# Decayed keys in a buffer of their own, made one chunk ahead of the scores

## The chip, the core and the metric

The kernel runs on one core of one Trainium2 chip. The metric is device time in microseconds (us). A kernel is timed in several runs, and the median counts. One more run is profiled; its rows are quoted below. Engines are named as the profile names them: PE (TensorE, matmuls) with PEld (its weight loads), DVE (VectorE), ACT (ScalarE), POOL (GpSimd) and SP (SyncE, which issues most of the DMAs).

## What is computed

Three stages follow one another: a linear attention with a decaying state, a dense feed-forward layer with SiLU, and a mixture of 8 experts of which each token takes one.

```python
def _attn_ref(q, k, v, alpha):            # batch 4, heads 8, seq 768, head_dim 48
    for t in range(S):
        state = alpha[:, :, t, :, None] * state + np.einsum('bhd,bhe->bhde', k[:, :, t], v[:, :, t])
        y[:, :, t] = np.einsum('bhd,bhde->bhe', q[:, :, t], state)

def _moe_ref(x, w_in, w_out):             # 3072 tokens, 384 -> 2048 -> 384
    h = x @ w_in
    return (h * (1.0 / (1.0 + np.exp(-h)))) @ w_out

def _moe2_ref(...):                       # token -> one of 8 experts, relu(x @ w1[e]) @ w2[e], times its gate
```

## The kernel before

The attention is cut into 24 chunks. Chunk n holds 128 positions of one of the 4 batches, for all 8 heads; n // 4 is the place in the sequence and n % 4 the batch. The feed-forward layer is cut into 8 blocks of 384 tokens, so a block uses the output of 3 chunks. Block 0 can start when its chunks are there, and from then on the attention of later chunks is mixed into the feed-forward work: `block` calls `pump_j` twice for each of the 16 pieces of a block, and each call takes one step of the generator `att_steps`. After the last block come the experts.

Matrix products of this kernel are made from two fp16 halves of each operand (a high part and a rest), three products for each pair; `qs`, `ss`, `vs`, `st` and `kd` are such pairs. The high part is a copy on ACT, the rest a subtraction on DVE or POOL.

A chunk n goes through these steps. `att_A` makes the running product P of the decays and its reciprocal R on DVE, and the end decay `pe` on POOL. `att_Bk` transposes k on PE into the PSUM tile `ptr` and multiplies it by R into `K` (L673, DVE). `att_Bq` does the like for `Q`, and splits it into `qs`. `att_C` makes the scores: 16 small matmuls `sc<-Q,K` (L717), copied to `S` by ACT (L727) and masked by POOL (L728). `att_S` splits the masked scores into `ss` (L740 on ACT, L741 on DVE). `att_KT` prepares the keys for the state: for chunks from `NF` = 6 on it multiplies `K` in place by the end decay (L754, POOL), splits the product into `kd` (L756 on ACT, L757 on POOL) and lets a DMA transpose it into `KT` (L759, queue of SP). `att_D` makes the output `yp` from `ss` and `vs` (L795) and from `qs` and the old state (L788). `att_U` makes `up<-vs,KT` (L829) and adds it to the state (L843, DVE). The last 4 chunks (20 to 23) need no new state, so `att_KT` and `att_U` return at once there.

Steps of two chunks are interleaved: after `att_C(n)` follow `att_A(n+1)`, `att_S(n)` with `att_KT(n)`, `att_Bk(n+1)`, `att_D(n)`, `att_Bq(n+1)` and `att_U(n)`.

The PSUM tiles of attention (`sc` twice, `ptr` three times, `yp`, `up`, so 7 for a chunk) take turns in 3 banks of the pool `ps_a`. The bank of `up` is that of the transposed k, so `up` of chunk n waits until `K` of chunk n+1 has been multiplied; the bank of the transposed q is that of the transposed decays, which R reads.

The order on each engine isn't the order of the code: a list scheduler places the instructions of all engines by its own estimate of when each could run. Each engine then works through its list in that order. The feed-forward matmuls are L900 (`mm1`) and L923 (`mm2`). `lead["a"]` is the latest ACT instruction that made the fp16 copy of a feed-forward piece; `behind(x, y)` holds x after y on the same engine.

At the end of a block `route` finds the expert of each token (many small DVE operations, a few on POOL, and a scatter by POOL, L990).

Of the kernel before, what the change touches and what calls it, by code (L numbers as in the profile page):

```python
# [8 lines left out]
FP32 = mybir.dt.float32  # L9
FP16 = mybir.dt.float16  # L10
I32 = mybir.dt.int32
ACTF = mybir.ActivationFunctionType
ALU = mybir.AluOpType
# [259 lines left out]
def attention_silu_moe_kernel(  # L273
# [14 lines left out]
    nc = tc.nc  # L288
    B, H, S, D = q.shape
# [4 lines left out]
    NPAIR = H // 2  # L294
    NCH = NT // 128
# [27 lines left out]
    def guard(kind, thr=0.0, op=ALU.is_lt):  # L323
# [16 lines left out]
        out=tri, in_=tri, pattern=[[1, 128]], compare_op=ALU.is_gt, fill=0.0, base=0, channel_multiplier=-1  # L340
# [32 lines left out]
    if True:  # L373
# [54 lines left out]
        NBUF, NF = 2, 6  # L428
# [52 lines left out]
        def behind(ins, before):  # L481
            tc.add_manual_dep(
                ins.ins, before.ins.name, mybir.DependencyInfo(mybir.DependencyClass.NoSync, mybir.DependencyReason.DATA),
                reason="an order within one engine",
            )
# [45 lines left out]
        gates, lead = {}, {}  # L531
# [94 lines left out]
        def att_load(n, names):  # L626
            if n >= NCH:
                return
            c, b = divmod(n, B)
            for nm in names:  # L630
                t = third[nm] if n == 2 else nat[nm][n % NBUF]
                nc.sync.dma_start(
                    out=t[:, :, 0:D], in_=att_src[nm][b, :, c * 128:(c + 1) * 128, :].rearrange("h p d -> p h d")
                )
                ch.setdefault(n, {})[nm] = t
# [4 lines left out]
        def transpose4(src):  # L640
            pt = bank([128, NPAIR, 128], FP32, "ptr")
            for p in range(NPAIR):
                nc.tensor.transpose(pt[:, p, :], src[:, p * 128:(p + 1) * 128], ident)
            return pt
# [24 lines left out]
        def att_Bk(n):  # L669
            d = ch[n]  # L670
            pk = transpose4(flat(d["k"]))
            K = a2.tile([128, NPAIR, 128], FP32, tag="K", name="K")
            ins = nc.vector.tensor_mul(out=K, in0=pk, in1=d["R"])  # L673
            if n == 2:
                lead[0] = ins
            d["K"] = K

# [65 lines left out]
        def att_KT(n):  # L743
            d = ch[n]
            if n // B == CPB - 1:
                return
            K = d["K"]
            if n < NF:
                pk = transpose4(K.rearrange("p a t -> p (a t)"))
                KT = d["KT"] = a2.tile([128, NPAIR, 128], FP32, tag="KT", name="KT32")  # L750
                nc.scalar.activation(out=KT, in_=pk, func=ACTF.Copy)
                return
            wide = d["pe"][:, 0].rearrange("r (p o) -> r p o", o=1).to_broadcast([128, NPAIR, 128])
            nc.gpsimd.tensor_tensor(out=K, in0=K, in1=wide, op=ALU.mult)  # L754
            kd = a2.tile([128, 2, NPAIR, 128], FP16, tag="kd", name="kd", bufs=1)
            nc.scalar.activation(out=kd[:, 0], in_=K, func=ACTF.Copy)  # L756
            nc.gpsimd.tensor_sub(out=kd[:, 1], in0=K, in1=kd[:, 0])  # L757
            KT = a2.tile([128, 2 * NPAIR, 128], FP16, tag="KT", name="KT")
            nc.sync.dma_start_transpose(out=KT, in_=kd.rearrange("p s a t -> p (s a t)"))  # L759
            d["KT"] = KT  # L760

        THREE = ((0, 0), (0, 1), (1, 0))

        def att_D(n, g):
            d = ch[n]
            c, b = divmod(n, B)
            if g == 0:
                d["y"] = bank([128, 512], FP32, "yp")[:, 0:H * D]
            yp = d["y"]
            if n >= NF:  # L770
                vs, ss = d["vs"], d["ss"]
            for p in (2 * g, 2 * g + 1):
                w = 2 * D * p
                if n < NF:
                    if c:
                        nc.tensor.matmul(
                            out=yp[:, w:w + 2 * D], lhsT=d["Q"][:, p, :], rhs=state[b][:, p, :], start=True, stop=False
                        )
                    for i in range(2):
                        cs = slice(w + i * D, w + (i + 1) * D)  # L780
                        nc.tensor.matmul(
                            out=yp[:, cs], lhsT=d["S"][i][:, p, :], rhs=flat(d["v"])[:, cs], start=(c == 0),
                            stop=(c == 0 or i == 1),
                        )
                    continue
                if c:
                    for m, (x, y) in enumerate(THREE):
                        nc.tensor.matmul(  # L788
                            out=yp[:, w:w + 2 * D], lhsT=d["qs"][:, x, p, :], rhs=d["st"][:, y, p, :],
                            start=(m == 0), stop=False,  # L790
                        )
                for i in range(2):
                    cs = slice(w + i * D, w + (i + 1) * D)
                    for m, (x, y) in enumerate(THREE):
                        nc.tensor.matmul(  # L795
                            out=yp[:, cs], lhsT=ss[:, i, x, p, :], rhs=vs[:, y, cs], start=(c == 0 and m == 0),
                            stop=(m == 2 and (c == 0 or i == 1)),
                        )
            if g == 1:
                ys = d["ys"] = a2.tile([128, 2, H * D], FP16, tag="ys", name="ys")  # L800
                lead[n - 1] = split(yp, SX / (SQ * SST), ys[:, 0], ys[:, 1])
# [49 lines left out]
        def att_steps():  # L851
            for n in range(3):
                att_load(n, "akqv")
            yield
            att_A(0)
            yield
            att_Bk(0)
            yield
            att_V(0)
            att_Bq(0)  # L860
            yield
            for n in range(NCH):
                more = n + 1 < NCH
                att_C(n)
                yield
                if more:
                    att_A(n + 1)
                    att_load(n + 3, "a")
                yield
                att_S(n)  # L870
                att_KT(n)
                yield
                if more:
                    att_Bk(n + 1)
                    att_load(n + 3, "k")
                    yield
                att_D(n, 0)
                yield
                att_D(n, 1)
                yield  # L880
                att_move(n)
                if more:
                    att_V(n + 1)
                    att_Bq(n + 1)
                    att_load(n + 3, "q")
                    yield
                att_U(n)
                if 0 < n < NF:
                    att_load(n + 2, "v")
                if n + 1 >= NF:  # L890
                    att_load(n + 3, "v")
                yield n
# [584 lines left out]
```

## Time and profile before

| what | us |
|---|---|
| median of 3 runs | 813.39 |
| lowest and highest run | 812.8, 814.5 |
| the profiled execution's own time | 813.08 |
| its span, first to last instruction | 811.4 |
| PE busy in the span | 753.4 |

The profiled execution took 1.7 us more than its span, which is start and end outside the instructions. In the rows below, "x16" counts instructions that a view has merged, a duration is that of the merged piece, and a bracket at the end of a row says how long the engine had stood idle before it and whose end released it. A matmul's end is modelled, and matmuls overlap: one starts while the one before it is still shown as busy.

### The profile page before, as it was taken

The numbers are of one execution on the slowest core, as the hardware profiler recorded it, in microseconds if no ns is written. First come the engines' busy times: TensorE is split into PE (matmuls) and PEld (weight loads), VectorE is DVE, ScalarE is ACT, GpSimd is POOL, SyncE is SP. The second block draws the span as 40 slices with busy tenths as digits, with TensorE's granted clock in tenths as the row PEclk, the third lists the DMA queues.
The fourth block names the chain that finished last, engine by engine and source line by source line (L and its number), as shares of the span: only waits on it lengthen the run. The fifth ranks groups of instructions, "written<-read, shape, count | busy, mean of one in ns | idle before, by whom it ended". The sixth has DMA issues, their size and how long they took to land. (4 is left out here: it accounts for less than half of the span.)

```text
span 811.4 us, 16634 instructions
## 1 busy us (share of the span) xinstructions
PE 753.4 (93%) x5614; PEld 472.3 (58%) x5614; DVE 504.3 (62%) x1452; ACT 423.9 (52%) x921; POOL 238.1 (29%) x330
## 2 busy tenths in 40 slices
PE   6788789999999899999999999989798999999996
PEld 5665467667666556665756655545354555555553
DVE  7699955587877888787887586576743222222221
ACT  2365635566766767676766675567623232222221
POOL 3351412263454554445233120030223011110101
PEclk9769979999999999999999999999899999999999
DMA  9997213044445535544431345246686666566662
GB/s 189 251 284 221 64 30 60 21 92 95 82 110 107 121 88 120 134 99 116 101 91 48 98 151 170 62 152 181 182 167 163 124 122 114 118 120 114 121 109 37
DMA packets 241100, 97.94 MB, mean 121 GB/s; under 512 B 222041, under 2 KB 230398, under 8 KB 240880
## 3 DMA queue, kind: packets, MB, share of 16 engines
q1 hardware_dynamic: 237424, 85.58, 48.6%
q0 software_dynamic: 3584, 11.18, 4.0%
q8 instruction: 51, 0.84, 0.4%
q14 instruction: 41, 0.34, 0.1%
HBM read 58.39 MB, written 12.16 MB: 87 GB/s over the span
## 5 line engine op out<-in xcount | busy, mean ns | idle before, releaser
L923 PE MATMUL o<-wo_h,w2l 128*128 128x392 f16 x528 | 147.2, 331 | 5.3 <-DVE wo_h L572 3.3
L900 PE MATMUL hp<-w2h,wi_h 128*128 128x384 f16 x576 | 145.4, 331 | 6.8 <-ACT w2l L907 3.0
L923 PEld LDWEIGHTS <-w2l 128*128 128x128 f16 x792 | 75.4, 99 | 54.7 <-issue 4.8
L1235 PE MATMUL hp<-w1h,xT 128*128 (+1 forms) x384 | 101.4, 383 | 5.5 <-DVE work L1242 5.5
L900 PEld LDWEIGHTS <-wi_h 128*128 128x128 f16 x768 | 73.8, 99 | 54.1 <-issue 9.6
L1242 DVE SCALAR_TENSOR_TENSOR work<-hp,work 128x512 f16<-128x512 f32 x56 | 38.6, 691 | 95.8 <-ACT work L1241 95.8
L900 PE MATMUL hp<-w2h,wi_l 128*128 128x384 f16 x288 | 94.2, 330 | 1.0 <-DVE wi_l L507 1.0
L923 PE MATMUL o<-wo_l,w2l 128*128 128x392 f16 x264 | 87.7, 332 | 0.0
L1235 PEld LDWEIGHTS <-xT 128*128 128x128 f16 (+1 forms) x576 | 50.4, 101 | 62.5 <-issue 8.6
L1274 POOL DMA_INDIRECT out_dram<-ob,mt x28 | 27.5, 981 | 169.6 <-ACT ob L1271 166.9
L923 PE MATMUL o<-wo_h,g 128*128 128x392 f16 x240 | 66.7, 331 | 1.7 <-ACT g L908 1.7
L1241 ACT ACTIVATE work<-hp 128x512 f16<-128x512 f32 x56 | 33.3, 596 | 61.7 <-PE hp L1235 59.9
L909 DVE SCALAR_TENSOR_TENSOR w2l<-w2l 128x384 f16<-128x384 f32 x88 | 50.7, 580 | 23.2 <-ACT w2l L908 21.9
L1235 PE MATMUL hp<-w1l,xT 128*128 (+1 forms) x192 | 64.5, 383 | 0.0
L907 ACT ACTIVATE w2l<-hp 128x384 f32<-128x384 f32 x88 | 42.2, 483 | 25.3 <-PE hp L900 21.9
L900 PEld LDWEIGHTS <-wi_l 128*128 128x128 f16 x384 | 37.8, 98 | 25.4 <-DVE wi_l L507 1.8
L923 PEld LDWEIGHTS <-g 128*128 128x128 f16 x360 | 34.5, 98 | 26.6 <-ACT g L908 2.6
L900 PE MATMUL hp<-w2l,wi_h 128*128 128x384 f16 x192 | 48.6, 326 | 0.0
L908 ACT ACTIVATE w2l<-w2l 128x384 f16<-128x384 f32 x88 | 45.3, 522 | 5.6 <-PE o L923 4.2
L1263 PEld LDWEIGHTS <-work 128*128 128x128 f16 (+1 forms) x384 | 33.3, 101 | 23.0 <-DMA work<-work 0.8
L703 POOL TENSOR_TENSOR qs<-Q,qs 128x512 f16<-128x512 f32 x18 | 21.5, 1195 | 85.0 <-ACT qs L702 85.0
L727 ACT ACTIVATE S<-sc 128x512 f32<-128x512 f32 x48 | 26.0, 593 | 35.8 <-PE sc L717 35.6
(281 smaller groups left out, 1603.1 us busy)
## 6 DMA issues: line engine op xcount, KB each, us to landing
work<-in_moe_w_dram SPq DMA_DIRECT2D x24, 512.0 KB, 3.7
work<-in_moe_w_dram SPq DMA_DIRECT2D x30, 384.0 KB, 3.3
w1h<-in_moe_w_in_dram SPq DMA_DIRECT2D x6, 768.0 KB, 5.3
nat_a<-in_alpha_dram SPq DMA_DIRECT2D x23, 192.0 KB, 3.0
nat_k<-in_k_dram SPq DMA_DIRECT2D x23, 192.0 KB, 3.7
nat_q<-in_q_dram SPq DMA_DIRECT2D x23, 192.0 KB, 3.4
nat_v<-in_v_dram SPq DMA_DIRECT2D x23, 192.0 KB, 3.0
w1h<-in_moe_w_out_dram SPq DMA_DIRECT2D x5, 768.0 KB, 8.0
```

The lines of the kernel that those rows point to most:

```text
L703: nc.gpsimd.tensor_sub(out=qs[:, 1], in0=Q, in1=qs[:, 0])
L727: nc.scalar.activation(out=s, in_=sc[i], func=ACTF.Copy, scale=SST if n >= NF else SST * SV)
L900: ins = nc.tensor.matmul(out=hp, lhsT=wi[a][f // 2][:, c, (f % 2) * 128:(f % 2 + 1) * 128], rhs=x[:, c, :], start=(n == 0), stop=(n == 3 * ...
L907: nc.scalar.activation(out=g, in_=hp, func=ACTF.Silu, scale=1.0 / (SX * SWI))
L908: lead["a"] = nc.scalar.activation(out=gh, in_=g, func=ACTF.Copy, scale=SG)
L909: lead["g"] = nc.vector.scalar_tensor_tensor(out=gl, in0=g, scalar=SG, in1=gh, op0=ALU.mult, op1=ALU.subtract)
L923: nc.tensor.matmul(out=acc[t], lhsT=a[:, ts], rhs=wo[w][f // 2][:, f % 2, :], start=(f == 0 and n == 0), stop=(f == KF - 1 and n == 2),)
L1235: nc.tensor.matmul(out=hp[ts], lhsT=xT[:, a, ts], rhs=w1s[w][c][:, e if isinstance(e, int) else bass.ds(e, 1), fs], start=(n == 0), stop=( ...
L1241: lead["a"] = nc.scalar.activation(out=hs[:, 0], in_=hp, func=ACTF.Relu)
L1242: lead["g"] = nc.vector.scalar_tensor_tensor(out=hs[:, 1], in0=hp, scalar=0.0, in1=hs[:, 0], op0=ALU.max, op1=ALU.subtract)
L1263: nc.tensor.matmul(out=po[ts], lhsT=hT[c // 4][:, at + ts.start:at + ts.stop], rhs=w2s[w][c][:, e if isinstance(e, int) else bass.ds(e, 1) ...
L1274: nc.gpsimd.indirect_dma_start(out=out[:, :], out_offset=bass.IndirectOffsetOnAxis(ap=d["row"], axis=0), in_=ob, in_offset=None, bounds_ch ...
```

## The change

`K` gets one buffer (it had two). The decayed keys get a tile `Kd` of their own instead of overwriting `K`. `att_Kd(n+1)` makes it on POOL right behind `att_Bk(n+1)`, so a chunk earlier than before. The split into `kd` and the DMA transpose (`att_kd(n+1)`) come behind the first half of `att_D(n)`, and the ACT copy in it is held behind `lead["a"]`. `att_KT` is left for the chunks below 6 alone.

```diff
--- before.py
+++ after.py
@@ -669,7 +669,7 @@
         def att_Bk(n):
             d = ch[n]
             pk = transpose4(flat(d["k"]))
-            K = a2.tile([128, NPAIR, 128], FP32, tag="K", name="K")
+            K = a2.tile([128, NPAIR, 128], FP32, tag="K", name="K", bufs=1)
             ins = nc.vector.tensor_mul(out=K, in0=pk, in1=d["R"])
             if n == 2:
                 lead[0] = ins
@@ -744,20 +744,24 @@
             d = ch[n]
             if n // B == CPB - 1:
                 return
-            K = d["K"]
-            if n < NF:
-                pk = transpose4(K.rearrange("p a t -> p (a t)"))
-                KT = d["KT"] = a2.tile([128, NPAIR, 128], FP32, tag="KT", name="KT32")
-                nc.scalar.activation(out=KT, in_=pk, func=ACTF.Copy)
-                return
+            pk = transpose4(d["K"].rearrange("p a t -> p (a t)"))
+            KT = d["KT"] = a2.tile([128, NPAIR, 128], FP32, tag="KT", name="KT32")
+            nc.scalar.activation(out=KT, in_=pk, func=ACTF.Copy)
+
+        def att_Kd(n):
+            d = ch[n]
+            Kd = d["Kd"] = a2.tile([128, NPAIR, 128], FP32, tag="Kd", name="Kd", bufs=1)
             wide = d["pe"][:, 0].rearrange("r (p o) -> r p o", o=1).to_broadcast([128, NPAIR, 128])
-            nc.gpsimd.tensor_tensor(out=K, in0=K, in1=wide, op=ALU.mult)
+            nc.gpsimd.tensor_tensor(out=Kd, in0=d["K"], in1=wide, op=ALU.mult)
+
+        def att_kd(n):
+            d = ch[n]
+            Kd = d.pop("Kd")
             kd = a2.tile([128, 2, NPAIR, 128], FP16, tag="kd", name="kd", bufs=1)
-            nc.scalar.activation(out=kd[:, 0], in_=K, func=ACTF.Copy)
-            nc.gpsimd.tensor_sub(out=kd[:, 1], in0=K, in1=kd[:, 0])
-            KT = a2.tile([128, 2 * NPAIR, 128], FP16, tag="KT", name="KT")
+            behind(nc.scalar.activation(out=kd[:, 0], in_=Kd, func=ACTF.Copy), lead["a"])
+            nc.gpsimd.tensor_sub(out=kd[:, 1], in0=Kd, in1=kd[:, 0])
+            KT = d["KT"] = a2.tile([128, 2 * NPAIR, 128], FP16, tag="KT", name="KT")
             nc.sync.dma_start_transpose(out=KT, in_=kd.rearrange("p s a t -> p (s a t)"))
-            d["KT"] = KT
 
         THREE = ((0, 0), (0, 1), (1, 0))
 
@@ -868,13 +872,19 @@
                     att_load(n + 3, "a")
                 yield
                 att_S(n)
-                att_KT(n)
+                if n < NF:
+                    att_KT(n)
                 yield
+                decayed = NF <= n + 1 < NCH - B
                 if more:
                     att_Bk(n + 1)
                     att_load(n + 3, "k")
+                    if decayed:
+                        att_Kd(n + 1)
                     yield
                 att_D(n, 0)
+                if decayed:
+                    att_kd(n + 1)
                 yield
                 att_D(n, 1)
                 yield
```

The scheduler then places the instructions anew. Line numbers behind the edit are up to 10 higher in the changed kernel.

On POOL, this is one chunk in the middle of a block (chunk 12), first before. `K<-K,pend` is the decay, `S<-S` are the two masks, `kd<-K,kd` is the rest of the split; `pend`, the state times its decay and `qs` belong to the next chunk already.

```order
L754 TENSOR_TENSOR K<-K,pend 128x512
L728 AFFINE_SELECT S<-S 128x512 x2
L664 TENSOR_SCALAR pend<-P 128x4 x2
L757 TENSOR_TENSOR kd<-K,kd 128x512
L838 TENSOR_TENSOR state_200<-state_200,pend 128x384
L703 TENSOR_TENSOR qs<-Q,qs 128x512
```

The same place in the changed kernel:

```order
L728 AFFINE_SELECT S<-S 128x512 x2
L664 TENSOR_SCALAR pend<-P 128x4 x2
L842 TENSOR_TENSOR state_200<-state_200,pend 128x384
L755 TENSOR_TENSOR Kd<-K,pend 128x512
L762 TENSOR_TENSOR kd<-Kd,kd 128x512
L703 TENSOR_TENSOR qs<-Q,qs 128x512
```

The masks now come first, and the decay and the split of the next chunk stand behind the state, ahead of `qs`.

On ACT, this is chunk 7 before; `S<-sc` are the scores, `junk` a check of P and of R, `w2l` the feed-forward pieces:

```order
L727 ACTIVATE S<-sc_1943 128x512
L727 ACTIVATE S<-sc_1944 128x512
L756 ACTIVATE kd<-K 128x512
L661 ACTIVATE junk,guard_decay<-P 128x512
L740 ACTIVATE ss<-S 128x512 x2
L661 ACTIVATE junk,guard_decay<-R 128x512
L907 ACTIVATE w2l_180<-hp 128x384
L908 ACTIVATE w2l_180<-w2l_180 128x384
L705 ACTIVATE st<-state_200 128x384
L506 ACTIVATE ys<-yp 128x384
L702 ACTIVATE qs<-Q 128x512
```

and in the changed kernel:

```order
L727 ACTIVATE S<-sc_1951 128x512
L727 ACTIVATE S<-sc_1952 128x512
L740 ACTIVATE ss<-S 128x512
L661 ACTIVATE junk,guard_decay<-P 128x512
L740 ACTIVATE ss<-S 128x512
L917 ACTIVATE w2l_180<-hp 128x384
L918 ACTIVATE w2l_180<-w2l_180 128x384
L661 ACTIVATE junk,guard_decay<-R 128x512
L761 ACTIVATE kd<-Kd 128x512
L705 ACTIVATE st<-state_200 128x384
L506 ACTIVATE ys<-yp 128x384
L683 ACTIVATE vs<-nat_v_198 128x384
```

The copy into `kd` has gone from its place ahead of both `ss` copies to one behind them, ahead of `st`, `ys`, `vs` and `qs`.

On POOL at the end of a block (behind the masks of chunk 13), where `route` (L951 to L990) is mixed in, before:

```order
L838 TENSOR_TENSOR state_201<-state_201,pend 128x384
L951 COPY row<-tok 128x1 x2
L980 TENSOR_TENSOR nx<-nx,half 128x1 x2
L974 TENSOR_SCALAR row<-nx 128x1 x2
L703 TENSOR_TENSOR qs<-Q,qs 128x512
L980 TENSOR_TENSOR nx<-nx,half 128x1
L990 DMA xs_d<-row,pos 25728x394 x2
L974 TENSOR_SCALAR row<-nx 128x1
L951 COPY row<-tok 128x1
L990 DMA xs_d<-row,pos 25728x394
```

and in the changed kernel:

```order
L842 TENSOR_TENSOR state_201<-state_201,pend 128x384
L961 COPY row<-tok 128x1 x2
L990 TENSOR_TENSOR nx<-nx,half 128x1 x2
L755 TENSOR_TENSOR Kd<-K,pend 128x512
L984 TENSOR_SCALAR row<-nx 128x1 x2
L762 TENSOR_TENSOR kd<-Kd,kd 128x512
L703 TENSOR_TENSOR qs<-Q,qs 128x512
L990 TENSOR_TENSOR nx<-nx,half 128x1
L1000 DMA xs_d<-row,pos 25728x394 x2
L984 TENSOR_SCALAR row<-nx 128x1
L961 COPY row<-tok 128x1
L1000 DMA xs_d<-row,pos 25728x394
```

Here `Kd` and the subtraction into `kd` come between the operations of `route`; the decay that stood behind the last scatter, ahead of the next masks, is gone.

On SP the transpose into `KT` stood between the loads of the decays and of k; now it stands behind the load of q. On PE no instruction is added or removed. Counted in the two orders, the feed-forward matmuls between the transposes of k and `up` are 8 or 9 in most chunks of the changed kernel and 11 in most chunks before; in chunks 9, 13, 17 and 18 they go from 11, 11, 7 and 18 to 12, 9, 14 and 23. PE's order differs from about the end of chunk 5 to the scores of chunk 20; behind these it is the same to the end of the program.

## Rows read from the trace of the kernel before

**Rows 1.** The page: PE's busy time, and its granted clock in 40 slices (tenths).

```profile
PE 753.4 (93%) x5614; PEld 472.3 (58%) x5614; DVE 504.3 (62%) x1452; ACT 423.9 (52%) x921; POOL 238.1 (29%) x330
...
PEclk9769979999999999999999999999899999999999
```

**Rows 2.** Stretches: PE, PEld, DVE, ACT, POOL busy us (instructions); clock, DMA, GB/s.

```profile
160.00:400.00 240.00, 232.27 (x2122) 156.69 (x2121) 195.77 (x529) 159.54 (x354) 114.20 (x153) 1.00 0.48 106
400.00:470.00 70.00, 70.00 (x587) 45.67 (x585) 50.38 (x146) 45.97 (x99) 16.28 (x28) 1.00 0.26 73
```

**Rows 3.** PE's waits, 160 to 400 us: us in total, times, longest.

```profile
PE up L829 <- DVE K L673: 3.1, 4, 1.1
PE pr L961 <- DVE state L843: 1.9, 2, 0.9
PE ptr L643 <- DVE R L658: 1.0, 2, 0.6
PE yp L795 <- DVE ss L741: 0.8, 1, 0.8
```

**Rows 4.** Instructions on the tile K: ns least/median/most, first and last start.

```profile
L754 POOL TENSOR_TENSOR K<-K,pend x14: 1041/1048/1751, 163.9 to 383.1; 128x512 f32<-128x512 f32 x14
...
L757 POOL TENSOR_TENSOR kd<-K,kd x14: 1149/1161/1169, 166.1 to 386.0; 128x512 f16<-128x512 f32 x14
```

**Rows 5.** Timeline of chunk 11: start us, us, instruction.

```profile
242.34 1.16 PE L717 MATMUL sc<-Q,K 64*128 64x128 f32 x16
...
243.59 1.04 POOL L754 TENSOR_TENSOR K<-K,pend 128x512 f32<-128x512 f32 x1 [2.17 <-PE sc L717]
...
243.93 0.33 PE L923 MATMUL o<-wo_h,w2l 128*128 128x392 f16 x1
...
244.26 0.49 PE L923 MATMUL o<-wo_h,w2l 128*128 128x392 f16 x2
244.59 1.23 POOL L728 TENSOR_SCALAR_AFFINE_SELECT S<-S 128x512 f32<-128x512 f32 x2
...
244.67 0.63 ACT L756 ACTIVATE kd<-K 128x512 f16<-128x512 f32 x1
...
247.10 0.62 ACT L740 ACTIVATE ss<-S 128x512 f16<-128x512 f32 x1
...
247.31 0.91 DVE L741 TENSOR_TENSOR ss<-S,ss 128x512 f16<-128x512 f32 x1
...
248.43 1.02 DVE L741 TENSOR_TENSOR ss<-S,ss 128x512 f16<-128x512 f32 x1
...
249.84 0.68 DVE L673 TENSOR_TENSOR K<-ptr,R 128x512 f32<-128x512 f32 x1
...
251.22 0.67 PE L829 MATMUL up<-vs,KT 128*128 128x96 f16 x12
```

**Rows 6.** Timeline of chunk 20, which makes no decayed keys.

```profile
396.33 1.16 PE L717 MATMUL sc<-Q,K 64*128 64x128 f32 x16
...
398.27 1.23 POOL L728 TENSOR_SCALAR_AFFINE_SELECT S<-S 128x512 f32<-128x512 f32 x2 [4.42 <-ACT S L727]
...
400.20 0.61 ACT L740 ACTIVATE ss<-S 128x512 f16<-128x512 f32 x1
...
401.27 0.68 DVE L741 TENSOR_TENSOR ss<-S,ss 128x512 f16<-128x512 f32 x1
...
403.13 0.69 DVE L673 TENSOR_TENSOR K<-ptr,R 128x512 f32<-128x512 f32 x1
```

**Rows 7.** Timeline of chunk 10: POOL beside DVE, and the state's sum.

```profile
231.00 1.15 POOL L757 TENSOR_TENSOR kd<-K,kd 128x512 f16<-128x512 f32 x1
...
231.21 1.50 DVE L741 TENSOR_TENSOR ss<-S,ss 128x512 f16<-128x512 f32 x1
...
240.39 0.72 DVE L843 SCALAR_TENSOR_TENSOR state<-up,state 64x192 f32<-64x192 f32 x2
```

**Rows 8.** Timeline of chunk 18: the longest wait of up.

```profile
376.27 0.67 PE L829 MATMUL up<-vs,KT 128*128 128x96 f16 x12 [1.08 <-DVE K L673]
```

## The prediction

> **What bounds the kernel now.** The page first: PE is busy for 753.4 of 811.4 us, at the upper clock level (2.4 GHz, full speed) in nearly all slices [rows 1], so a change gains only where PE still stands idle. From the two orders the edit reaches from the end of chunk 5 (about 140 us) to the scores of chunk 20 (396 us), so I asked for the busy time of the stretch 160 to 400 us. There PE works 232.27 of 240 us: 7.73 us of idle time is what the page's count leaves to gain. In the 70 us behind it, chunks 20 to 23, PE is never idle, with feed-forward and attention mixed as before [rows 2]. DVE (195.77 of 240) and POOL (114.20) have room on the mean.
>
> PE's waits in this stretch name the causes: `up` waits four times, 3.1 us in all, for `K` of the next chunk; the transposes wait for R twice, 1.0; `yp` waits once for `ss`, 0.8; and `pr`, the count of `route`, waits twice for DVE, 1.9 [rows 3]. The longest is the 1.08 us ahead of `up` in chunk 18 [rows 8]. A wait costs a little more than its idle row: two matmuls that are 0.33 us long each fill 0.49 us together, so one starts 0.16 us behind the other and the modelled end of the last one hides 0.17 us of each wait [rows 5].
>
> So DVE's chain to `K` is late in some chunks. The timeline of chunk 11 shows what stands in it, in us from the start of the scores at 242.34. POOL takes the decay first (1.25 to 2.29), and the masks come behind it (2.25 to 3.48). ACT takes the copy into `kd` at 2.33. The second `ss` copy starts at 4.76, DVE's second `ss` ends at 7.11, `K` at 8.18, and `up` starts at 8.88 [rows 5].
>
> Chunk 20 is the same chunk without decayed keys: masks from 1.94 to 3.17, the second `ss` copy at 3.87, the second `ss` done at 5.62, `K` done at 7.49 [rows 6]. That is about what the edit should make of the other chunks, and this trace holds it already; but chunk 20 also lacks `up` and the state's product on POOL, so it flatters a little.
>
> **The change part by part.**
>
> *Decay away from the masks, copy away from `ss`.* 14 decays of 1.05 us leave POOL's place ahead of the masks, and 14 copies of 0.63 us leave ACT's place ahead of `ss` [rows 4, 5]. Masks could start when the scores are copied, about 0.3 us sooner in the middle of a block, by a whole decay at the start of one, where POOL is behind with the scatters. From chunk 11 to chunk 20 the second `ss` is done 7.11 - 5.62 = 1.49 us sooner and `K` 8.18 - 7.49 = 0.69 us sooner [rows 5, 6].
>
> *What the scheduler makes of it.* In most chunks it puts `up` 3 feed-forward matmuls nearer to the transposes of k (11 to 8), so PE asks for `K` 3 x 0.163 = 0.49 us sooner. Against 0.69 that leaves 0.20 us more room, not 0.69, on top of the 0.70 that chunk 11 has (8.88 - 8.18) [rows 5]. The four waits of `up` lie in chunks 9, 13, 17 and 18, and the counts there go from 11, 11, 7, 18 to 12, 9, 14, 23. With `K` at least 0.69 us sooner the room grows by 0.69 + 0.16 = 0.85, 0.69 - 0.33 = 0.36, 0.69 + 1.14 = 1.83 and 0.69 + 0.82 = 1.51 us. The largest wait is 1.08 + 0.17 = 1.25 us, in chunk 18 [rows 8]; the other three share 3.1 - 1.08 = 2.0, about 0.67 + 0.17 = 0.84 each [rows 3]. Chunks 9, 17 and 18 are covered. In chunk 13 some 0.5 us is left by this sum; there masks and splits run beside `route`, and the copy and the decay that go are worth up to 1.05 + 0.63, so I count it half. Bounds for `up`: 2.6 to 3.8 us gained; I take 3.5.
>
> *The other waits.* `yp` on `ss` (0.8 + 0.17) goes if `ss` is 1.49 us sooner and asked for 5 matmuls (0.8 us) sooner at most: 0.97. The two waits of the transposes on R (1.0 + 0.34) go with the `ss` that DVE no longer waits for in between; from 0 to 1.34, I take 0.9. `pr` on DVE (1.9) is `route`'s own work, which the edit leaves: 0. Sum of the gains: 3.5 + 0.97 + 0.9 = 5.4 us.
>
> *The moved pieces.* `Kd` (1.05) and the subtraction (1.16) now run on POOL behind `K`, beside DVE's second half of the chunk (the splits of `st`, `vs` and the feed-forward pieces). No row of before shows them there. From below the cost is 0, if they fall beside DVE work that doesn't mind. From above: in chunk 10 a DVE split that began 0.21 us into POOL's subtraction took 1.50 us [rows 7], against 0.68 for the same form in chunk 20 [rows 6], so a collision costs DVE 0.82, and two in each chunk 1.64. DVE's second half must end before the next scores, since these wait for the state's sum: in chunk 10 it ended at 241.11 and the scores began at 242.34, so 1.23 us of room [rows 5, 7]. With the 0.49 that the order draws together, 0.74 are left, and 1.64 - 0.74 = 0.90 us for each chunk would be PE's wait. The old collisions beside `ss` go in exchange. I take 0.9 us over the whole stretch, one chunk's worth, since a full double collision in every chunk needs DVE's two splits to meet both POOL pieces each time.
>
> The Trainium skill's page "SBUF — State Buffer", section "Who interferes with whom", says that a VectorE operation with two inputs in SBUF and a GpSimd operation that reads SBUF exclude each other for the whole instruction. The 1.50 us of the split agrees with it: it ended 0.56 us behind POOL's subtraction. By that rule every two-input split that starts under `Kd` or under the subtraction waits for its end, which is the slower rival below: with the row's collision counted for one chunk the median comes to 808.9, by the rule in half of the chunks to 814.3.
>
> *At no cost.* One buffer for `K`: its next writer comes behind the scores that read it and behind `Kd`, a chunk earlier; the cover is the rest of a chunk. `Kd` and `kd` are refilled once a chunk. The transpose DMA moves behind the load of q on SP; its `KT` is asked for a chunk later than it is made, so it has several us more than before. On ACT, `kd` holds up `st`, `ys`, `vs` and `qs` until `Kd` is done, at about 7.5 + 1.05 = 8.6 us of the chunk; the outputs that `ys` copies are complete at about that time, so this hides, and if not, the price is that of a late state (above). At a block's end `Kd` and the subtraction, 2.2 us, stand in `route`'s list on POOL; before, a decay stood ahead of the masks behind it, so about 1 us of it is paid back.
>
> Sum: 813.08 (the profiled execution) - 5.4 + 0.9 = 808.6. The median lies 0.3 above the profiled execution, so 808.9 for a median.
>
> **The rivals.**
>
> *Slower: DVE's second half becomes late.* Every chunk's splits meet `Kd` and the subtraction, the state's sum comes late, and the next scores wait. For it: DVE is busy for 82% of the stretch, and the room in chunk 10 is only 1.23 us. Against it: three of the four kinds of waits of before lie ahead of `K`, none at the scores [rows 3]. Price: up to 0.90 us a chunk; with half of the 14 chunks caught, 6.3 us. It decides from 5.4 / 14 = 0.39 us a chunk. Time: 813.4 - 5.4 + 6.3 = 814.3, and 820.6 at the full price.
>
> *No change.* The scheduler uses up the room that it sees, so that new waits take the place of the old ones. For it: 0.49 of the 0.69 us are spent at once. Against it: chunk 20 has the order that most chunks now get (8 matmuls from its transposes of k to those of q), without idle time on PE [rows 2, 6]. Time: 813.2.
>
> *All of it.* PE becomes as dense as behind 400 us, `pr` included: 7.73 idle plus 9 times 0.17 is 9.3 us. For it: the clean stretch [rows 2]. Against it: the waits of `pr`. Time: 804.1.
>
> That the edit doesn't do what it says is excluded by the order: the masks do come first.
>
> **How the numbers follow.** Forecast (a gain of 1.7 to 7 us, 806.4 to 811.7) 0.50; all of it 0.10; no change 0.24; slower 0.16. 0.2%, 1.6 us, is about what a measurement can tell from no change. Faster has the first two, 0.60. The range should leave out 2 in 10 at most: from 804.5, which cuts the far end of the full gain, to 815.0, which takes in the slower rival at half price and cuts it at the full one.
>
> **What the new profile would show.** Masks that start at 1.9 to 2.0 us of a chunk, the second `ss` done at about 6, `K` at 7.5, and rows of `up` waiting for `K` gone or below 1 us in all; PE idle in 160 to 400 us down from 7.7 to 3 or 4. The slower rival would show PE's scores (L717) waiting for the state's sum, and splits of 1 us and more beside `Kd`. The prediction is wrong if `K` comes no sooner, because DVE does other work there instead, or if the block ends lose on POOL what the middles gain.

## The result and the profile after

The changed kernel takes 816.21 us (median of 20 runs, 814.14 to 823.23), the kernel before 810.48 in the same series (20 runs, 805.3 to 815.15). The ratio is 1.0079, with a 95% interval of 1.0055 to 1.0102 (the two medians alone give 1.0071): slower by 0.8%, where the forecast was some 0.5% faster. The forecast counted from 813.39 us, a median of 3 runs. The profiled execution took 819.28 us, with a span of 817.6 us, 6.2 us longer than before.

PE's line of the page answers to [rows 1]: the same busy time, in a longer span.

```profile
PE 753.2 (92%) x5614; PEld 472.5 (58%) x5614; DVE 501.2 (61%) x1452; ACT 423.3 (52%) x921; POOL 239.9 (29%) x330
...
PEclk9669979999999999999999999999899999999998
```

The two stretches of [rows 2], with the same columns:

```profile
160.00:400.00 240.00, 225.76 (x2054) 151.15 (x2053) 187.62 (x516) 153.51 (x344) 108.36 (x147) 0.99 0.46 99
400.00:470.00 70.00, 70.00 (x573) 45.74 (x572) 51.32 (x148) 46.88 (x101) 19.59 (x32) 1.00 0.29 79
```

PE now idles 14.24 us between 160 and 400 us, 6.51 more than before, about the 6.2 us of span. The stretch behind it is as dense as it was. PE's waits from 160 to 400 us, as in [rows 3]:

```profile
PE yp L799 <- DVE ss L741: 10.1, 10, 2.4
PE pr L971 <- DVE ys L507: 1.1, 1, 1.1
PE up L833 <- DVE K L673: 0.7, 1, 0.7
...
PE ptr L643 <- DVE R L658: 0.5, 3, 0.2
```

What the forecast wanted gone did shrink: `up` waits 0.7 us for `K` (3.1 before), `ptr` 0.5 for R (1.0), `pr` 1.1 (1.9). But `yp` now waits ten times for `ss`, 10.1 us in all, where it waited once for 0.8.

The timeline shows why. First chunk 7, whose scores begin at 176.30, then chunk 11 (scores at 241.43), the chunk of [rows 5]:

```profile
176.30 1.16 PE L717 MATMUL sc<-Q,K 64*128 64x128 f32 x16
...
178.18 1.23 POOL L728 TENSOR_SCALAR_AFFINE_SELECT S<-S 128x512 f32<-128x512 f32 x2 [2.10 <-ACT S L727]
...
181.80 0.68 DVE L741 TENSOR_TENSOR ss<-S,ss 128x512 f16<-128x512 f32 x1
...
183.30 0.69 DVE L673 TENSOR_TENSOR K<-ptr,R 128x512 f32<-128x512 f32 x1
...
184.68 0.67 PE L833 MATMUL up<-vs,KT 128*128 128x96 f16 x12
...
237.16 1.21 DVE L580 SCALAR_TENSOR_TENSOR w1l<-work,w1h 128x1024 f16<-128x1024 f32 x1
...
237.54 1.85 POOL L762 TENSOR_TENSOR kd<-Kd,kd 128x512 f16<-128x512 f32 x1 [1.32 <-ACT kd L761]
...
239.41 1.23 SPq L764 DMA_TRANSPOSE KT<-kd  x1
...
240.74 0.53 SPq L592 DMA_DIRECT2D work<-in_moe_w_dram  x1
241.16 0.55 DVE L919 SCALAR_TENSOR_TENSOR w2l<-w2l 128x384 f16<-128x384 f32 x1
241.36 1.21 SPq L810 DMA_TRANSPOSE w2h<-ys  x1
...
241.43 1.16 PE L717 MATMUL sc<-Q,K 64*128 64x128 f32 x16
...
246.81 0.22 DVE L597 TENSOR_REDUCE guard_w<-work 128x1 f32<-128x64 f32 x1 [5.10 <-DMA work<-in_moe_w_dram]
246.95 1.36 DVE L651 TENSOR_TENSOR_SCAN P<-ptr,pmin 128x128 f32<-128x128 f32 x4
...
249.21 1.16 DVE L741 TENSOR_TENSOR ss<-S,ss 128x512 f16<-128x512 f32 x1
...
250.43 0.20 PE L799 MATMUL yp<-vs,ss 128*128 128x48 f16 x1 [2.37 <-DVE ss L741]
```

In chunk 7 all goes as the prediction described: masks from 1.88 us of the chunk, the second `ss` done at 6.18, `K` at 7.69, `up` at 8.38. In chunk 11 the masks are early as well, but DVE is not there to use it. The instruction that holds it is one that the prediction does not name: L597, a reduction of 0.22 us on a freshly loaded piece of w1 (an expert weight, fetched in this stretch for the stage behind it). With the like reduction of v (L689) it belongs to the guards, the kernel's own range test of its inputs. DVE works through its list in order, so from 241.71 to 246.81 the scan to P, both `ss` splits and `K` stand behind a reduction whose result nobody is waiting for. P starts at 5.52 us of the chunk instead of 1.84, and `yp` waits 2.37 us. The ten waits of `yp` lie in six chunks, 9, 11, 12, 13, 15 and 16, and in each of them DVE had stood at guards for 1.7 to 5.1 us; chunk 14 had 2.0 us of it without a wait of `yp`.

DVE's waits from 160 to 400 us, first in the changed kernel, then in the kernel before:

```profile
DVE guard_w L597 <- DMA work<-in_moe_w_dram: 13.7, 5, 5.1
DVE st L706 <- ACT st L705: 8.0, 7, 2.5
DVE guard_nat L689 <- DMA nat_v<-in_v_dram: 6.7, 3, 3.2
...
DVE P L651 <- PE ptr L643: 4.7, 3, 2.0
```

```profile
DVE P L651 <- PE ptr L643: 14.0, 9, 2.9
DVE guard_nat L689 <- DMA nat_v<-in_v_dram: 6.7, 4, 2.2
...
DVE guard_w L597 <- DMA work<-in_moe_w_dram: 4.8, 6, 1.3
```

The two guards held DVE for 11.5 us before and for 20.4 now. And the slack that could swallow it, the time in which DVE waited for PE ahead of P anyway, fell from 14.0 to 4.7 us.

PE also asks sooner now. The first `yp` matmuls of chunk 11 that read `ss`, first in the kernel before, then in the changed one:

```profile
248.94 0.21 PE L795 MATMUL yp<-vs,ss 128*128 128x48 f16 x2
```

```profile
247.19 0.21 PE L799 MATMUL yp<-vs,ss 128*128 128x48 f16 x2
```

They start 6.60 us behind the start of the scores before and 5.76 now, so a late DVE has 0.84 us less. In chunk 12 it is 8.82 before and 6.07 now: there DVE stood at the two guards for 3.26 us before and 2.80 now, but only the changed kernel's `yp` waits.

### The profile page after: what moved, and what is told of

Its sections match the earlier page's. It is cut to its first block, busy times and chain, and to the rows that moved or that the text cites. A ratio compares the mean times of both kernels' runs of the same rounds, so it can differ in the third digit from the quotient of the medians.

```text
span 817.6 us, 16631 instructions
## 1 busy us (share of the span) xinstructions
PE 753.2 (92%) x5614; PEld 472.5 (58%) x5614; DVE 501.2 (61%) x1452; ACT 423.3 (52%) x921; POOL 239.9 (29%) x330
## 5 line engine op out<-in xcount | busy, mean ns | idle before, releaser
L728 POOL TENSOR_SCALAR_AFFINE_SELECT S<-S 128x512 f32<-128x512 f32 x48 | 34.3, 737 | 48.8 <-ACT S L727 48.6
L1273 PE MATMUL po<-w2h,work 128*128 (+1 forms) x256 | 43.6, 326 | 0.3 <-DMA work<-work 0.2
```

What stands on the lines that cost most here:

```text
L728: nc.gpsimd.affine_select(out=s, in_=s, pattern=[[0, NPAIR], [1, 128]], compare_op=ALU.is_ge, fill=0.0, base=0, channel_multiplier=-1,)
L1273: nc.tensor.matmul(out=po[ts], lhsT=hT[c // 4][:, at + ts.start:at + ts.stop], rhs=w2s[w][c][:, e if isinstance(e, int) else bass.ds(e, 1) ...
```

## The experiments

Theory 1 is what was just read: DVE stands at the guards. Its rivals: theory 2, the copy into `kd` on ACT, ahead of `st`, delays DVE's second half (`st` waits 8.0 us); theory 3, `Kd` and the subtraction on POOL stretch DVE's splits, which is the slower rival of the prediction. Each kernel is compared with the kernel before on the same chip. The expected times were set against 810.5 and 816.2 us. On the chips of these runs the kernel before took 812.6 to 813.8, so the same ratio means a time 2 to 3 us higher; where the two readings differ, both are given, "by the ratio" being the ratio times 810.48. The scheduler places all instructions anew after any edit, so each run moves more than its edit.

In the table, "load waits" are DVE's waits at the guards of w1 and v, and "yp" are PE's waits of `yp` for `ss`, both from 160 to 400 us, in us, of the one profiled execution of each kernel.

| kernel | ratio to before, 95% interval | load waits, w1 + v | yp |
|---|---|---|---|
| before | 1 | 4.8 + 6.7 | 0.8 |
| changed | 1.0079 (1.0055 to 1.0102) | 13.7 + 6.7 | 10.1 |
| e1 changed, guards behind | 0.9912 (0.9881 to 0.9944) | 0 | 0.3 |
| e2 before, guards behind | 0.9941 (0.9915 to 0.9967) | 0 | 0.9 |
| e3 changed, transpose late | 1.0043 (1.0015 to 1.0070) | 5.2 + 8.2 | 5.7 |
| e4 changed, copy on POOL | 0.9976 (0.9953 to 1.0000) | 3.3 + 7.8 | 4.7 |
| e5 own buffer only | 1.0016 (0.9989 to 1.0043) | 6.9 + 6.4 | 5.3 |
| e6 changed, w1 guard behind | 1.0011 (0.9989 to 1.0034) | 0 + 11.5 | 5.1 |
| e7 changed, v guard behind | 1.0027 (0.9993 to 1.0062) | 12.7 + 0 | 5.0 |
| e8 changed, guards behind, copy on POOL | 0.9903 (0.9869 to 0.9936) | 0 | 0 |
| e9 changed, w1 load on ACT | 1.0065 (1.0038 to 1.0092) | 9.9 + 6.5 | 8.3 |
| e10 changed, no such guards | 0.9909 (0.9883 to 0.9935) | none | 0 |
| e11 before, no such guards | 0.9911 (0.9885 to 0.9938) | none | 0.4 |
| e12 before, guards behind, copy on POOL | 0.9891 (0.9871 to 0.9912) | 0 | 1.1 |

### Do the guards cost the time? (e1, e2, e6, e7)

The edit of e1 ties each reduction behind the split that reads the same load, so that it can no longer stand ahead of it:

```diff
-                    split_after(st, SW1, w1s["h"][c][:, e, :], w1s["l"][c][:, e, :])
+                    rest = split_after(st, SW1, w1s["h"][c][:, e, :], w1s["l"][c][:, e, :])
                     if c == 0:
-                        nc.vector.tensor_reduce(
+                        behind(nc.vector.tensor_reduce(
                             out=guard("w1", 2.0 ** -6), in_=st[:, 0:64], axis=AXX, op=ALU.max, apply_absolute_value=True
-                        )
+                        ), rest)
...
+                    if nm == "v" and n >= NF:
+                        behind(ins, rest)
```

> The changed kernel, with two small reductions on DVE (the guards of w1 and of v, L597 and L689) held behind the split that reads the same load. Theory 1 (DVE's list stands at these reductions for loads that now come later, because the transpose into KT stands ahead of them on SP): DVE's waits for these loads fall from 20.4 us in 160 to 400 us to under 5, yp's waits for ss from 10.1 to under 4, and the time falls by 5 to 8 us from the changed kernel's 816.2, to 808 to 811. Theory 2 (ACT's kd copy stands ahead of st and waits for Kd, so DVE's second half is late: st waits 8.0 us) and theory 3 (Kd and the subtraction on POOL stretch DVE's splits): within 1.5 us of 816.2, yp's waits stay at 8 us or more.

Measured: 0.9912 (median 806.72, before 812.77), 1.7% below the changed kernel's ratio and better than expected. PE's busy time from 160 to 400 us and its wait of `yp` in e1:

```profile
160.00:400.00 240.00, 235.23 (x2180) 159.96 (x2177) 200.60 (x542) 164.14 (x362) 110.57 (x151) 1.00 0.52 107
```

```profile
PE yp L802 <- DVE ss L744: 0.3, 2, 0.2
```

PE's idle time falls from 14.24 to 4.77 us. This is theory 1; by theories 2 and 3 nothing should have happened, since the copy on ACT and POOL's pieces stay where they are (`st` still waits 6.2 us for ACT here).

e2 is the same edit on the kernel before.

> The kernel before, with the same two reductions held behind the split of the same load. Theory 1: they wait for their loads there too (4.8 and 6.7 us), but yp waited only 0.8 us for ss, so the time stays within 1.6 us of 810.5. If the reductions cost the kernel before as much as the changed one, 5 us or more would be gained here as well, and they would not be the difference between the two.

Measured: 0.9941 (807.97). Neither branch met it: 0.6% is more than the 1.6 us allowed and a little less than the 5 us of the other branch. So the guards cost the kernel before too, about a third of what they cost the changed one by this edit (0.6% against 1.7%), and about half of it by e10 and e11 below (0.9% against 1.7%).

e6 keeps the first half of that edit, for w1, and e7 the second, for v.

> The changed kernel with only the guard of w1 (L597) held behind the split of its load. Theory 1: DVE's waits at it (13.7 us, five times) go, those of v's guard (6.7) stay; the two longest waits of yp, in chunks 11 and 12, go; 808 to 812. Theory 2 and 3: within 1.5 us of 816.2.

> The changed kernel with only the guard of v (L689) held behind the split of v. Theory 1: DVE's waits for v (6.7 us, three times) go, those for w1 (13.7) stay; some 3 us are gained, 811 to 815, less than with the guard of w1 alone.

Measured: 1.0011 (814.72) and 1.0027 (813.54). e7 is within its range. e6 is above its own by the time, and inside it by the ratio (811.4), but v's wait didn't stay as expected: it grew from 6.7 to 11.5 us. In e7 w1's wait stayed at 12.7. Each alone gives 0.5 to 0.7%, both together 1.7%.

### What is the change worth without them? (e10, e11)

e10 and e11 leave out the guards of w1 and of v in the late chunks, and with them a part of the range test, from the changed kernel and from the kernel before.

```diff
-                    if c == 0:
-                        nc.vector.tensor_reduce(
-                            out=guard("w1", 2.0 ** -6), in_=st[:, 0:64], axis=AXX, op=ALU.max, apply_absolute_value=True
-                        )
...
-                for nm in "qkv":
+                for nm in "qk" if n >= NF else "qkv":
```

> The changed kernel without the guards of w1 and of v of the late chunks: this leaves out a part of the kernel's own range test of its inputs, some 20 reductions of 0.2 us. Theory 1: the same as with the guards held behind the splits, 805 to 809, some 10 us below the changed kernel, though the reductions themselves are 4 us of DVE in all.

> The kernel before without the same guards; the same part of the range test is left out. Beside the run above it shows the change with DVE's list free of loads: with the forecast's steps right the changed one is 2 to 6 us faster, so 808 to 812 here; if the change has no worth of its own the two are within 1.6 us.

Measured: 0.9909 (806.25) and 0.9911 (805.75). e10 came as expected (2 us better by the ratio), and e11 met the second branch: the two medians are 0.5 us apart, the changed kernel's the higher. With six runs each and intervals of about 2 us either way, the forecast's 5.4 us are out, while a worth of 1 or 2 us is not. The other two pairs agree: e1 and e2 (0.9912 and 0.9941, intervals that overlap), and e8 and e12 below, where the changed kernel's ratio is the higher. PE's waits for `ss`, `K` and `KT` in e11:

```profile
PE up L825 <- DVE K L669: 1.3, 3, 0.6
PE up L825 <- DMA KT<-kd: 1.3, 2, 1.0
PE yp L791 <- DVE ss L737: 0.4, 1, 0.4
```

`up` waits for `K` 1.3 us here instead of 3.1, and another 1.3 for `KT`. So more than half of the wait for `K` that the change was to win back goes with the guards, while the decay still stands ahead of the masks. The timeline of DVE in the kernel before shows it in two of the four chunks where `up` waited, 9 (scores at 203.72) and 13 (at 272.32):

```profile
206.67 0.20 DVE L689 TENSOR_REDUCE guard_nat<-nat_v 128x1 f32<-128x48 f32 x1 [1.20 <-DMA nat_v<-in_v_dram]
206.79 1.36 DVE L651 TENSOR_TENSOR_SCAN P<-ptr,pmin 128x128 f32<-128x128 f32 x4
...
279.01 0.22 DVE L597 TENSOR_REDUCE guard_w<-work 128x1 f32<-128x64 f32 x1 [1.00 <-DMA work<-in_moe_w_dram]
279.15 0.81 DVE L658 TENSOR_TENSOR R<-ptr,R 128x128 f32<-128x128 f32 x2
```

In chunk 9 the guard of v stands right ahead of P, in chunk 13 that of w1 between the reciprocal and the products for R, and each keeps DVE idle for 1.0 to 1.2 us on the way to `K`. Small DVE operations of `route` stand ahead of `K` there as well. In chunk 17 they stand there alone, and in chunk 18 the guard of v was done before P's input came.

### Why do the guards wait longer in the changed kernel? (e3, e5, e9, e4)

For each of the six loads of w1 in this stretch that a guard reads, the wait is: how late the load is issued behind the split that frees its buffer, plus its way to landing, less the time from that split until DVE's list reaches the guard. Summed over the six, worked out from the timelines (a load for which DVE did not wait is counted as landed when the guard starts):

| us, six loads | before | changed | e9 | e3 | e4 |
|---|---|---|---|---|---|
| load issued late | 0.2 | 2.5 | 0.2 | 0.6 | 0.8 |
| issue to landing | 22.8 | 26.9 | 26.4 | 25.0 | 25.6 |
| from the split until DVE reaches the guard | 18.2 | 15.7 | 16.7 | 20.4 | 23.0 |
| wait | 4.8 | 13.7 | 9.9 | 5.2 | 3.3 |

Of the 9 us that came on top, 2.3 are a load that stood on SP behind the transpose into `KT`: all of it is chunk 11, where the buffer was free at 238.38 and SP issued the load at 240.74, behind the transpose at 239.41. That transpose had waited for POOL's subtraction (L762), which took 1.85 us beside DVE's split of w1, 0.7 more than its median of 1.16. Another 4.1 us is slower landing, of which chunk 11 has 2.5 (6.07 us for 3.59). The last 2.5 us is the guard's own place: DVE reaches it sooner behind the split than before. With late issue and slow landing, chunk 11 alone makes more than half of the 9.

e3 moves the transpose alone back behind the scores of its own chunk.

```diff
-            nc.sync.dma_start_transpose(out=KT, in_=kd.rearrange("p s a t -> p (s a t)"))
+            d["kd"] = kd
+
+        def att_turn(n):
...
+            nc.sync.dma_start_transpose(out=KT, in_=d.pop("kd").rearrange("p s a t -> p (s a t)"))
...
                 if n < NF:
                     att_KT(n)
+                elif n < NCH - B:
+                    att_turn(n)
```

> The changed kernel, with only the DMA transpose into KT moved back to where it was issued before, behind the scores of its own chunk. Theory 1: loads on SP no longer stand behind the transpose; DVE's waits for the loads of w1 and v fall from 20.4 us to the 11.5 of before or less, and the time to 809 to 813. Theory 2 and 3: within 1.5 us of 816.2.

Measured: 1.0043 (814.79). DVE's waits:

```profile
DVE guard_nat L689 <- DMA nat_v<-in_v_dram: 8.2, 3, 3.9
...
DVE guard_w L597 <- DMA work<-in_moe_w_dram: 5.2, 5, 2.0
```

The loads of w1 are on time again, the waits for v grew to 8.2 us, and about half of the loss is won back by the ratios, whose intervals overlap; the time is above the expected range, by 1 us or 2. The table says why w1's guard waits less: little of it is landing (25.0 for 26.9), most is the guard's place in the new order (20.4 for 15.7).

e9 takes the loads off SP:

```diff
-                nc.sync.dma_start(out=st, in_=w1[e, c * 128:(c + 1) * 128, :])
+                nc.scalar.dma_start(out=st, in_=w1[e, c * 128:(c + 1) * 128, :])
```

> The changed kernel with the loads of w1 (L592) issued from ACT's queue in place of SP's, so that they stand behind no transpose there. If the place on SP makes them late, DVE's waits at w1's guard fall from 13.7 us to 5 or less and the time to 812 to 815, as with that guard held behind. If the loads are late because they land slower beside the transposes, wherever they are issued, the waits stay at 10 us or more and the time at 815 to 818. The waits for v stay in both cases.

Measured: 1.0065 (818.00), not told from the changed kernel, and the waits came out at 9.9 us, all but in the second branch. Its profiled execution took 823.29 us, near its slowest. Two rows of w1's guard in e9:

```profile
245.57 0.22 DVE L597 TENSOR_REDUCE guard_w<-work 128x1 f32<-128x64 f32 x1 [0.45 <-DMA work<-in_moe_w_dram]
...
265.11 0.22 DVE L597 TENSOR_REDUCE guard_w<-work 128x1 f32<-128x64 f32 x1 [3.69 <-DMA work<-in_moe_w_dram]
```

The first is chunk 11: 0.45 us instead of 5.10, so that wait did come from the place on SP: issued at 241.81, it landed after 3.76 us, with the next transpose 1.0 us behind it. The second is chunk 12, where the load is issued at once behind its split in both kernels, with a transpose 3.4 us ahead of it and another 0.6 us behind. It landed 5.55 us later here and 3.99 us later in the changed kernel, so the wait grew from 2.13 to 3.69 us. Over the six loads e9 takes away the late issue (0.2 us for 2.5) and not the landing (26.4 us for 26.9). This agrees with the Trainium skill's page "DMA: Bandwidth & Descriptors", section "Issuing engines are not separate DMA queues": transfers run on the same 16 DMA engines whichever engine starts them, so another queue saves issue time alone.

That the transposes are what makes the landing slow rests on rows, and no run isolates it. For it: in the kernel before, chunk 13's load, issued 2.1 us behind a transpose, took 4.55 us and the other five 3.5 to 3.9. Against a simple rule: chunk 12's load took 3.99 and 5.55 us at the same distances from its transposes.

e5 leaves the code at its old place and changes only the buffers.

```diff
                 if n < NF:
                     att_KT(n)
+                elif n < NCH - B:
+                    att_Kd(n)
+                    att_kd(n)
```

> The decayed keys in a buffer of their own and one buffer for K, but the code of the decay, the split and the transpose at its old place, behind the scores of its own chunk. In the order the scheduler still puts the decay ahead of these scores, behind the state, since nothing but the buffer held it. If the buffer alone makes the change, the profile shows the changed kernel's pattern (transposes early on SP, DVE's waits for loads above 12 us, yp waiting 5 us or more for ss) and 813 to 818; if the place in the code matters, it comes out like the kernel before, 809 to 812.

Measured: 1.0016 (813.33), with load waits of 6.9 + 6.4 us and 5.3 us of `yp`: the pattern is that of the changed kernel at a smaller size. The time is in the first range, in the second by the ratio (811.8), and the interval takes in both no change and 0.4% slower, so e5 doesn't settle it. The buffer alone does let the decay go ahead of the scores, as the order in e5 shows: `Kd` at 178.85 us, the scores at 184.15. What the place in the code adds isn't shown.

e4 makes the copy into `kd` on POOL.

```diff
-            behind(nc.scalar.activation(out=kd[:, 0], in_=Kd, func=ACTF.Copy), lead["a"])
+            nc.gpsimd.tensor_copy(out=kd[:, 0], in_=Kd)
```

> The changed kernel, with the fp16 copy of Kd into kd on POOL in place of ACT, right behind Kd. Theory 2: st's waits for ACT fall from 8.0 us to under 2, yp's waits for ss fall with them, and the time falls by 4 us or more, to 812 or less. Theory 1: st waits less too, but DVE still stands at the reductions for their loads, and KT comes a copy of about 1 us later; 815 to 819. Theory 3 (POOL beside DVE): some 1 us more POOL work in each of 14 chunks beside DVE's second half, so slower than 816.2, 818 or more.

Measured: 0.9976 (811.81), which is theory 2's number; theory 3's is out. But the load waits fell as well:

```profile
DVE guard_w L597 <- DMA work<-in_moe_w_dram: 3.3, 5, 1.2
DVE st L706 <- ACT st L705: 1.4, 3, 0.8
```

So e4 alone doesn't tell theory 1 from theory 2. It does show that the length of the load waits isn't all: they come to 11.1 us, as before (11.5), and `yp` waits 4.7 us against 0.8. PE asks for `ss` 5.8 us behind the start of the scores in most chunks here, as in the changed kernel.

### Is anything left for the other theories? (e8, e12)

e8 is e1 with e4's copy on POOL, e12 the same two edits on the kernel before, where the copy reads `K`:

```diff
-            nc.scalar.activation(out=kd[:, 0], in_=K, func=ACTF.Copy)
+            nc.gpsimd.tensor_copy(out=kd[:, 0], in_=K)
```

> The changed kernel with both guards held behind the splits, and the copy into kd on POOL. Theory 1: the copy gained in the earlier run because kd, and with it the transposes on SP, came sooner; with the guards out of the way nothing is left to gain, so the same as with the guards alone within 2 us: 805 to 809. Theory 2 (ACT's copy ahead of st costs DVE by itself): st's waits (6.2 us with the guards alone) go and 3 us more are gained: 802 to 805.

> The kernel before with both guards held behind the splits and the copy into kd on POOL, to set beside the changed kernel with the same two edits (0.9903 of the kernel before). There the copy stands on POOL between the decay and the masks, about 1 us more ahead of the masks of each chunk; if the masks' place matters as the prediction had it, 809 to 813, 4 us or more above the changed one; if not, 804 to 808.

Measured: 0.9903 (804.19) and 0.9891 (803.40). e8's time is in theory 2's range, but its ratio is 0.0009 from that of e1 (0.9912), with intervals of 0.003 either way, and `st` still waits 2.0 us for ACT (6.2 in e1). So whether the copy on ACT costs up to 3 us of its own stays open; it isn't what made the changed kernel slow, since e1 keeps it there and loses the slowdown. e12 is as fast as e8, below its lower range, and 0.5% below e2, with intervals that don't meet: so the copy's place is worth something in the kernel before. It isn't an earlier `ss`: in the first full chunk the second `ss` is done at 8.35 us in e12 and at 7.46 in e2, but `up` starts at 10.66 us in e12 and at 8.89 in e2. The order there leaves DVE more room, and in no chunk does `up` wait for `K`. The masks on POOL, in the first full chunk of e8 (scores at 172.93) and then of e12 (scores at 173.32):

```profile
174.80 1.23 POOL L731 TENSOR_SCALAR_AFFINE_SELECT S<-S 128x512 f32<-128x512 f32 x2 [3.66 <-ACT S L730]
```

```profile
175.56 0.64 POOL L731 TENSOR_SCALAR_AFFINE_SELECT S<-S 128x512 f32<-128x512 f32 x1
...
176.72 0.63 POOL L731 TENSOR_SCALAR_AFFINE_SELECT S<-S 128x512 f32<-128x512 f32 x1
```

The masks are done at 3.10 us of the chunk in e8 and at 4.03 in e12, and the time is the same. When the masks come, inside this margin, doesn't show at the end.

e1, e2, e8, e10, e11 and e12 all beat both kernels, by 0.6 to 1.1% over the kernel before; of those that keep the guards, e8 and e12 have the lowest ratios.

## Why the prediction was wrong

**Where it failed.** The sum has no term for DVE's waits at loads. They were in the trace of before, 11.5 us from 160 to 400 us, and were not read; they rose to 20.4. The failed step is the list "At no cost": "The transpose DMA moves behind the load of q on SP; its `KT` is asked for a chunk later than it is made, so it has several us more than before." That named who waits for `KT`, and not what stands behind the transpose on SP or lands beside it, nor who waits for that: the loads of w1 and v, and behind them the guards in DVE's list. For the guard of w1 the transpose's issue is one chunk's 2.3 us. The other two parts, 4.1 us of slower landing and 2.5 of the guards' new place, stay open as to their cause.

A second term has the wrong sign: "`yp` on `ss` (0.8 + 0.17) goes if `ss` is 1.49 us sooner and asked for 5 matmuls (0.8 us) sooner at most". PE does ask 0.8 us sooner. But where DVE stands at a guard, `ss` comes later, and where 0.97 us of gain was put, `yp` waits 9.3 us more. Waits of the old length cost more in the new order, as e4 shows. The prediction's own sign of being wrong, that `K` comes no sooner, came true in such chunks (11.94 us of chunk 11, 8.18 before), only that DVE did no other work there: it stood.

**The gain.** Three of the four places were right: `up` waits 2.4 us less (3.5 with the hidden share was forecast), `ptr` 0.5 less, `pr` 0.8 less where 0 was put. But e10 and e11 show no such gain at the end once the guards are gone on both sides; that is what the rival "No change" had, by which the scheduler uses up the room that it sees. The term that is too large is "`K` at least 0.69 us sooner", taken from chunk 20. `K` and `up` of chunk 7, which no guard disturbs, in the kernel before (scores from 176.08):

```profile
183.46 0.68 DVE L673 TENSOR_TENSOR K<-ptr,R 128x512 f32<-128x512 f32 x1
...
184.97 0.67 PE L829 MATMUL up<-vs,KT 128*128 128x96 f16 x12
```

`K` is done at 8.06 us before and at 7.69 in the changed kernel, 0.37 sooner; `up` starts at 8.89 and at 8.38, 0.51 sooner. So the room between them doesn't grow by 0.20 us, it shrinks by 0.14. The step "DVE's chain to `K` is late" was right; its cause, the decay ahead of the masks, was taken from chunk 11, where `up` didn't wait. In chunks 9 and 13, two of the four where it did, a guard stood in the chain.

**What went as forecast.** In an undisturbed chunk masks, `ss` and `K` come at the times given. `kd` on ACT does hold up `st`, and e10 shows that this hides from `yp`: `st` waits 7.0 us there, and `yp` never waits for `ss`.

**The slower rival.** Its number, 814.3, is close to the 816.2 measured, but not by its mechanism: no wait of L717 for the state's sum stands among PE's waits. The collisions are there. The median of DVE's split of the old state (L706), first before, then in the changed kernel (ns least/median/most):

```profile
L706 DVE TENSOR_TENSOR st<-state,st x14: 533/556/1025, 170.9 to 393.2; 128x384 f16<-128x384 f32 x14
```

```profile
L706 DVE TENSOR_TENSOR st<-state,st x14: 544/1053/1387, 172.4 to 399.7; 128x384 f16<-128x384 f32 x14
```

It nearly doubled, which agrees with the rule cited in the prediction from the Trainium skill's page "SBUF — State Buffer", section "Who interferes with whom". But in e10 the median is still 1050 ns, in e11 it is 555, and the two take the same time, so the collisions of the splits alone cost nothing that these runs can tell. A share they do have: the longer subtraction of chunk 11 held back the transpose, and with it the load.

**Still open.** No run keeps the changed order and takes only the transposes away from the loads, so the 4.1 us of slower landing is put down to them from rows alone, and not all rows fit. Nor does a run keep the changed order and give PE its old distance to `ss`, so how the 9.3 us of `yp` divide between longer load waits and less room isn't shown. Since each edit makes the scheduler place everything anew, a difference of one or two tenths of a per cent between two of these kernels is not put down to a cause.

## What to carry to other kernels

Before a DMA is moved in a queue, list what stands behind it there and which in-order engine waits for that, however small the waiting instruction is: 0.22 us of reduction held DVE for 5.1 us. An instruction that needs only a load is placed by a scheduler's guess of that load; tie it behind the work that needs the load anyway. And when a wait is to be removed, read what held the chain in the very chunk that waited, since a neighbour that didn't wait may show another cause.

## What the runs showed of the hardware

A load of w1 (512 KB) landed 3.6 us after its issue when the next transpose was issued 1.5 us behind it, as before at 238.95, and 6.07 us after it with a transpose 1.3 us ahead and another 0.6 us behind, in the changed kernel at 240.74. At one pair of distances, 3.4 us ahead and 0.6 us behind, it took 3.99 us in one run and 5.55 in another, so the transposes alone don't fix it. The prediction had no term for transfers beside each other.
